# q's last 64 columns: phi before the turn, and the turn on VectorE instead of TensorE

## The chip, the core and the metric

The kernel runs on one core of one Trainium2 chip. The core has a matrix engine (TensorE, PE in the profile; PEld is its weight load), three engines for elementwise work (VectorE is DVE, ScalarE is ACT, GpSimd is POOL), and SyncE (SP), which here issues DMAs. Each engine works through its own queue in order. The metric is the time of one execution on the device in microseconds, as the median of several runs.

## The reference

`x` has 2048 tokens of 576 columns. It is normalised (layer norm without weights), and then feeds two branches whose results are combined as `x + s * silu(g)`.

```python
qkv = xn @ wqkv                       # 576 -> 3 * 576, 32 heads of 18 columns
phi = lambda t: where(t > 0, t + 1, exp(t)) + 1e-6
kv  = einsum("bhsd,bhse->bhde", phi(k), v)      # over all tokens
z   = phi(k) summed over the tokens
num = einsum("bhqd,bhde->bhqe", phi(q), kv)
den = einsum("bhqd,bhd->bhq", phi(q), z) + 1e-6
s   = (num / den) @ wo
g   = (gelu(xn @ w_gate) * (xn @ w_up)) @ w_down    # 576 -> 4608 -> 576
out = x + s * silu(g)
```

What the change touches is `phi(q)` for the last 64 of the 576 columns of q. `phi(t)` is computed as max(t, 0) + 1e-6 + exp(min(t, 0)).

## The kernel before

The 2048 tokens are four blocks of 512 (`tb` 0 to 3), a block is four tiles of 128 tokens (`TT` is 4). All is in f32; a product is made from operands that are split into a rounded word (`hi`, by ScalarE) and its remainder (`lo`, by VectorE). The work goes through these stages:

- k and v by tiles, tokens in partitions: for tile t, `x_mm` makes three products of 416, 412 and 388 columns. The last one (`TW[2]`, 388) holds 324 columns of v and, behind them, the last 64 columns of q (`Q4` is 64). `k_post` makes phi(k), `v_post` (line 486) copies v and q out of PSUM. `place(t + 1)` prepares the operands of the next tile in the midst of tile t: `normalize` (line 247) subtracts and scales on VectorE, then ScalarE writes the rounded word `xo_B` and VectorE the remainders. Every second tile, `kv_pair` accumulates kv.
- q by groups, features in partitions: q has five groups (`NHG`). Groups 0 to 3 are products over a whole block, 128 rows of q by 512 tokens. They hold 126 columns of q each, and two of the last columns as two extra rows. Group 4 is the last 64 columns. These have come out of the token tiles with tokens in partitions, so they must be turned.
- after the q of blocks 0 and 1 (called stages (tb, group) here, in the lists `behind`, line 1534) come tiles 8 to 15 of k and v, then the q of blocks 2 and 3 (lists `ahead`, line 1566), then for each block the denominators (`den`, line 753), the scaling of phi(q) by them (`scale`, `halve`) and the product with kv and `wo` (`s_mm`, line 803).
- the gated feed-forward branch, by far the longest stage, from about 240 us on.

Group 4 works like this. For each tile, `v_post` writes the 64 columns twice, side by side, into `qt[tb]` (512 tokens by 2 x 64 columns). `q_mm` with `gi == NHG - 1` lets TensorE turn the four 128x128 pieces of `qt` into one PSUM bank, so that the 64 features stand in partitions 0 to 63 and again in 64 to 127. Then `phi` (line 410) runs as for the other groups, from the bank: ScalarE takes max(-t, 0) into `e`, VectorE takes max(t, 0) + 1e-6 into `ph`, ScalarE takes the exponential of `e`, GpSimd adds.

The order within each engine is the program's order: every helper (`act` at line 123, `vec` at 126, `mm` at 129, `pool` at 132, `dma` at 135) pins its instruction. The lists `behind` and `ahead` say what is issued after each group of q. For blocks 0 and 1, phi(q) goes to DRAM (`q_store`) and is fetched again later; for blocks 2 and 3 it stays in SBUF (`q_hold`). Buffers rotate under tags: six PSUM banks (`bank`), six tiles of the tag `gl` (among them `qt` and the stored `ph`), four of the tag `tmp` (among them `e`).

For the place of things in time: block 0's group 4 is at 53 us, in tile 5; block 1's at 83 us, behind group 0 of block 0; block 2's at 178 us, behind its own group 0; block 3's at 198 us, behind its own group 0 and behind `den(2)`. The differences of operands (`difference`, names `xf_B`) run on VectorE in the stages (0,0) and (2,0), and `kv_wo` (names `kw`, `kvh`, `kvl`) in the stages (2,1) to (2,3). `den(2)` multiplies phi(q) with z on TensorE (`d`), VectorE adds and inverts (`r`), ScalarE and VectorE write the words `aux`, and `scale(2, 0, 1)` spreads them over the partitions on TensorE (`b`).

Of the kernel before, what the change touches and what calls it, by code (L numbers as in the profile page):

```python
# [8 lines left out]
F32 = mybir.dt.float32  # L9
# [3 lines left out]
ALU = mybir.AluOpType  # L13
# [3 lines left out]
P = 128  # L17
# [74 lines left out]
def block_kernel(ctx, tc, x, xe, xt, wq_d, wkv_d, wo, wgu_d, wd_d, out):  # L92
# [12 lines left out]
    def big(i, shape, dt, name):  # L105
        return sb.tile(shape, dt, tag=f"b{i}", bufs=1, name=name)
# [7 lines left out]
    def gl_tile(shape, name, dt=F32):  # L114
        return sb.tile(shape, dt, tag="gl", bufs=6, name=name)

    def tmp(shape, name):
        return sb.tile(shape, F32, tag="tmp", bufs=4, name=name)
# [3 lines left out]
    def act(*args, **kw):  # L122
        pin(nc.scalar.activation(*args, **kw))  # L123

    def vec(op, *args, **kw):
        pin(getattr(nc.vector, op)(*args, **kw))  # L126

    def mm(*args, **kw):
        pin(nc.tensor.matmul(*args, **kw))  # L129

    def pool(op, *args, **kw):
        pin(getattr(nc.gpsimd, op)(*args, **kw))  # L132

    def dma(out, in_, eng=None):
        tc.keep_in_program_order((eng or nc.sync).dma_start(out=out, in_=in_))
# [33 lines left out]
    def spread(n0, n):  # L169

        bn = sb.tile([P, TT, 12], F32, tag="bn", bufs=2, name=f"bn_{n0}")
        mv = sb.tile([P, 2 * TT, 2], F32, tag="mv", bufs=4, name=f"mv_{n0}")
        for t in range(n):
            xs = xstat[(n0 + t) // 2][:, (n0 + t) % 2]
            for j in range(2):
                src = xs[:, j, 0:HALF] if n0 < TT else xs[:, j * HALF : (j + 1) * HALF]
                vec("bn_stats", out=bn[:, t, 6 * j : 6 * j + 6], in_=src)
            vec("bn_aggr", out=mv[:, t, :], in_=bn[:, t, :])
        st = sb.tile([P, 6, TT], F32, tag="st", bufs=4, name=f"st_{n0}")
        act(st[:, 0, 0:n], mv[:, 0:n, 1], AF.Ln, bias=eps_t)  # L180
        act(st[:, 2, 0:n], st[:, 0, 0:n], AF.Exp, scale=-0.5)
        vec("tensor_scalar", st[:, 1, 0:n], mv[:, 0:n, 1], LN_EPS, None, op0=ALU.add)
        mom[n0] = n, mv, st
# [130 lines left out]
    def difference(s, i):  # L314
        f = xf[s]
        nm, a, b, o = SUMS[i]
        vec("tensor_sub", f[o], f[a], f[b])
        f[nm] = f[o]
# [79 lines left out]
    def q_part(j, i, cs):  # L398
        return wq_l[:, j, cs] if i == 4 else wq[j][:, i, cs]
# [10 lines left out]
    def phi(o, src, name):  # L410

        e = tmp(list(o.shape), f"e_{name}")
        act(e, src, AF.Relu, scale=-1.0)
        vec("tensor_scalar", o, src, 0.0, EPS, op0=ALU.max, op1=ALU.add)
        act(e, e, AF.Exp, scale=-1.0)
        pool("tensor_add", o, o, e)
# [69 lines left out]
    def v_post(t, c):  # L486

        if c == 1:
            vas[t] = slot([P, 2 * NHG, P // 2], F32, f"va_{t}")
            pool("memset", vas[t][:, :, 0:1], 1.0)  # L490
        va, src = vas[t], pkv[t, c]
        n = D - TW[0] if c == 1 else 0
        g = 4 * c - 4
        act(
            va[:, g : g + 4, 1 : GW // 2 + 1],
            src[:, n : n + 2 * GW].rearrange("p (g j) -> p g j", g=4), AF.Copy,
        )
        if c == 2:
            act(
                va[:, 8:10, 1 : W4 // 2 + 1],  # L500
                src[:, 2 * GW : 2 * GW + W4].rearrange("p (g j) -> p g j", g=2), AF.Copy,
            )
            tb, i = divmod(t, TT)
            if i == 0:
                qt[tb] = gl_tile([P, TT, 2, Q4], f"qt_{tb}")
            act(
                qt[tb][:, i], src[:, None, 2 * GW + W4 : TW[2]].to_broadcast([P, 2, Q4]), AF.Copy,
            )

    def run(todo, n=None):  # L510
        for _ in range(len(todo) if n is None else min(n, len(todo))):
# [25 lines left out]
    def kv_pair(t):  # L537

        pair = [i for i in (t - 2, t - 1) if i in vas]
        for groups in (range(4), (4,)):  # L540
            for i in pair:
                kv_mm(i, groups)
        for i in pair:
            del pks[i], vas[i]
# [3 lines left out]
    def q_mm(tb, gi, o):  # L548
        s, b = divmod(tb, 2)
        pq = bank(f"q_{tb}_{gi}")  # L550
        if gi == NHG - 1:
            t = qt.pop(tb)
            for i in range(TT):
                pin(nc.tensor.transpose(
                    pq[:, i * P : (i + 1) * P], t[:, i].rearrange("p r j -> p (r j)"), ident
                ))
        else:
            n = 0
            for j, nm in enumerate(BS[b]):
                for wi, xi, rows in PASSES:  # L560
                    mm(
                        pq, q_part(j, wi, slice(gi * P, (gi + 1) * P)), xo[s][nm][:, xi, :],
                        start=(n == 0), stop=(n == 2 * len(PASSES) - 1),
                    )
                    n += 1
        phi(o, pq, f"q{tb}_{gi}")

    def q_store(tb, gi):
        if tb not in ph_d:
            ph_d[tb] = dr.tile([P, NHG, TBN], F32, name=f"phd_{tb}")  # L570
        o = gl_tile([P, TBN], f"ph_{tb}_{gi}")
        q_mm(tb, gi, o)
        dma(out=ph_d[tb][:, gi, :], in_=o)

    def q_hold(tb, i, gi):
        if tb not in ph:
            ph[tb] = big(i, [P, NHG, TBN], F32, f"ph_{tb}")
        q_mm(tb, gi, ph[tb][:, gi, :])
# [87 lines left out]
    def kv_wo(gi):  # L666

        if gi == 4:
            at["kvh"] = big(4, [P, 4, D], F32R, "kvh")
            at["kvl"] = big(5, [P, 4, D], F32R, "kvl")  # L670

            at["kv4"] = big(6, [P, 4, D], F32R, "kv4")
            pool("memset", at["kv4"][Q4:P, 1, :].bitcast(F32), 0.0)
        kvh, kvl, kv4 = at["kvh"], at["kvl"], at["kv4"]
        zc, mh = at["zc"], at["maskh"]
        wdt, k = (W4, P // 2 + W4 // 2 + 1) if gi == 4 else (GW, P)
        w = at["wo4"] if gi == 4 else at["wo"][:, gi]
        pw = []
        for c, cs in enumerate((slice(0, HALF), slice(HALF, D + 2))):
            pw.append(bank(f"kw_{gi}_{c}"))  # L680
            mm(
                pw[c][0:wdt, 0 : cs.stop - cs.start], at["kvm"][0:k, gi, 0:wdt], w[0:k, cs],
                start=True, stop=True,
            )
        r, x_ = slice(0, Q4 if gi == 4 else GW), slice(Q4, W4)
        z = pw[1][:, HALF : HALF + 1]

        def parts(hi, lo, rows):
            for c in range(2):
                cs = slice(c * HALF, (c + 1) * HALF)  # L690
                split(hi[:, cs], lo[:, cs], pw[c][rows, 0:HALF])

        if gi == 4:
            vec("tensor_copy", zx[x_], z[x_])
            parts(kv4[x_, 2, :], kv4[x_, 3, :], x_)
            for c in range(2):
                act(kv4[Q4:P, 0, c * HALF : (c + 1) * HALF], pw[c][r, 0:HALF], AF.Copy)

        vec(
            "tensor_scalar", zc[r, gi, :], mh[r, gi, :], z[r], None, op0=ALU.mult,  # L700
        )
        if gi == 4:
            parts(kv4[r, 0, :], kv4[r, 1, :], r)
        else:
            parts(kvh[r, gi, :], kvl[r, gi, :], r)
# [773 lines left out]
    for n in range(3, 2 * TT):  # L1479
        ends = []  # L1480
        if n < 2 * TT - 2:
            ends.append(lambda n=n: x_next(n + 2))
        if n >= TT:
            j, c = divmod(n - TT, 2)
            prep_q(c, j)
            if n == TT + 1:
                load_q(1)
        if n == 2 * TT - 1:
            ends += [lambda i=i: difference(0, i) for i in range(3)]
        kv_tile(n, end=ends)  # L1490
        if n in (4, 6):
            load_x(n + 4, 2)
        if n == TT:
            for nm in BS[0]:
                keep(0, nm, xo[0][nm])
        if n == TT:
            q_store(0, 4)
        if n == TT + 3:
            keep(0, "B22", xo[0]["B22"])

# [19 lines left out]
    def form_apart(nm):  # L1520
# [12 lines left out]

    behind = {
        (0, 0): [
            lambda: kv_pair(N0), lambda: q_store(1, 4), lambda: spread(N0, 2),
            lambda: difference(0, 3),
        ],
        (0, 1): [lambda: scales(N0), lambda: form("T1")],
        (0, 2): [lambda: form_apart("T3")],  # L1540
# [8 lines left out]
    for n in range(N0, 2 * N0):  # L1549
# [13 lines left out]
        if n == 2 * N0 - 1:  # L1563
# [1 line left out]
        kv_tile(n, late_, ends)  # L1565
    ahead = {
        (2, 0): [
            lambda: kv_pair(2 * N0), kv_done, lambda: q_hold(2, 7, 4), spread_sel,
            lambda: difference(1, 3),
        ],  # L1570
        (2, 1): [lambda: kv_wo(4)],
        (2, 2): [lambda: kv_wo(0), lambda: kv_wo(1), move_rows],
        (2, 3): [lambda: kv_wo(2), lambda: kv_wo(3)],
        (3, 0): [lambda: den(2), lambda: q_hold(3, 8, 4)],
        (3, 1): [lambda: scale(2, 0, 1), lambda: halve(2, 0, 1)],
        (3, 2): [lambda: scale(2, 2, 3), lambda: halve(2, 2, 3)],
        (3, 3): [lambda: scale(2, 4), lambda: halve(2, 4)],
# [114 lines left out]
```

## Time and profile before

| | |
|---|---|
| runs | 1454.80, 1455.42, 1455.93 us; median 1455.42 us |
| profiled execution | 1454.71 us, span 1453.0 us |
| granted TensorE clock | 1.000 |
| instructions | 22169 |
| busy: PE, DVE, ACT, POOL | 1446.4, 1146.2, 565.5, 579.3 us |

Busy time by stage, from the view by stretches of time:

```profile
core 0: us, PE busy (x) PEld busy (x) DVE busy (x) ACT busy (x) POOL busy (x), PEclk, DMA share, GB/s
0.00:77.00 77.00, 75.10 (x504) 70.93 (x505) 54.19 (x135) 37.84 (x93) 28.51 (x51) 1.00 0.58 215
77.00:115.00 38.00, 37.70 (x214) 32.57 (x213) 34.60 (x55) 20.46 (x36) 14.98 (x11) 1.00 0.48 178
115.00:172.00 57.00, 56.96 (x405) 55.55 (x404) 40.47 (x100) 22.10 (x57) 16.38 (x27) 1.00 0.32 109
172.00:215.00 43.00, 42.95 (x309) 35.52 (x308) 31.87 (x55) 25.10 (x52) 19.38 (x16) 1.00 0.04 13
215.00:560.00 345.00, 345.00 (x1763) 294.93 (x1763) 247.39 (x349) 114.50 (x201) 164.62 (x136) 1.00 0.37 131
560.00:1453.00 893.00, 888.68 (x5087) 799.50 (x5085) 737.66 (x920) 345.48 (x483) 335.40 (x280) 1.00 0.54 179
```

Each line is a stretch (start and end in us from the start of the span), its length, and then for each engine its busy time and its number of instructions. Tiles 0 to 7 lie in the first stretch, the q of blocks 0 and 1 in the second, tiles 9 to 15 in the third, the q of blocks 2 and 3 in the fourth.

In a timeline, a row gives the start in us, the duration (of several instructions together, where "x" says more than one), engine, line, operation, names written and read, shapes, and in brackets the idle time of the engine before it with what ended it. In a row of a group, "busy, mean ns" come after the bar. In the view of waits, the numbers are the total in us, how often, and the longest.

### The profile page before, as it was taken

The numbers are of one execution on the slowest core, as the hardware profiler recorded it, in microseconds if no ns is written. First come the engines' busy times: TensorE is split into PE (matmuls) and PEld (weight loads), VectorE is DVE, ScalarE is ACT, GpSimd is POOL, SyncE is SP. The second block draws the span as 40 slices with busy tenths as digits, with TensorE's granted clock in tenths as the row PEclk, the third lists the DMA queues.
The fourth block names the chain that finished last, engine by engine and source line by source line (L and its number), as shares of the span: only waits on it lengthen the run. The fifth ranks groups of instructions, "written<-read, shape, count | busy, mean of one in ns | idle before, by whom it ended". The sixth has DMA issues, their size and how long they took to land.

```text
span 1453.0 us, 22169 instructions
## 1 busy us (share of the span) xinstructions
PE 1446.4 (100%) x8272; PEld 1289.0 (89%) x8272; DVE 1146.2 (79%) x1609; ACT 565.5 (39%) x918; POOL 579.3 (40%) x520
## 2 busy tenths in 40 slices
PE   9999999999999999999999999999999999999998
PEld 8989989988888888888888888888889999999998
DVE  7688667376787887887777878777878978989898
ACT  6444365333232233322332232332236555545454
POOL 3342440225756567565575755667632000000000
PEclk9999999999999999999999999999999999999999
DMA  5554115621532315224242343324289887767886
GB/s 224 187 205 152 45 42 201 225 93 51 174 102 95 130 54 186 87 95 145 77 149 87 102 145 109 113 84 136 115 277 343 265 262 254 246 183 238 277 290 224
DMA packets 119237, 235.04 MB, mean 162 GB/s; under 512 B 11658, under 2 KB 45322, under 8 KB 117210
## 3 DMA queue, kind: packets, MB, share of 16 engines
q1 hardware_dynamic: 116330, 221.37, 45.2%
q0 software_dynamic: 2656, 12.06, 2.2%
q8 instruction: 65, 1.06, 0.3%
q14 instruction: 42, 0.34, 0.1%
q10 hardware_dynamic: 144, 0.20, 0.0%
HBM read 150.96 MB, written 82.58 MB: 161 GB/s over the span
## 4 chain that ended last, share of the span: by engine, by line
PE 97%; DVE 1%; ACT 1%; issue 0%; POOL 0%; DVEq 0%; ACTq 0%; POOLq 0%
PE bd L129 25%; PE al L887 16%; PE de L887 16%; PE ga L887 16%; PE kv L129 8%; PE be L887 8%; PE s L129 4%; PE q L129 3%; PE kv_a L129 1%; PE idle L129 0%; PE d L129 0%; PE kw L129 0%; PE b L129 0%; ACT e_q L123 0%; PE xt L241 0%
## 5 line engine op out<-in xcount | busy, mean ns | idle before, releaser
L132 POOL TENSOR_TENSOR sm<-raw 128x384 f32<-128x384 f32 x72 | 75.0, 1042 | 144.3 <-DMA raw<-in_wgu_dram 113.3
L129 PE MATMUL kv<-wkv,xo_B 128*128 128x412 f32 (+2 forms) x662 | 125.0, 347 | 0.3 <-ACT xo_B L123 0.3
L129 PEld LDWEIGHTS kv<-wkv,xo_B 128*128 128x128 f32 x662 | 120.3, 188 | 1.7 <-ACT xo_B L123 0.8
L126 DVE TENSOR_TENSOR wa<-sm,wa 128x768 fp32r<-128x768 f32 x72 | 92.2, 1281 | 36.1 <-ACT wa L123 35.2
L129 PE MATMUL bd<-w_head,hi 128*128 128x288 f32 x516 | 118.0, 294 | 0.0
L126 DVE TENSOR_TENSOR wb<-raw,wb 128x256 fp32r<-128x256 f32 (+1 forms) x108 | 101.2, 937 | 7.4 <-ACT wb L123 5.8
L126 DVE TENSOR_TENSOR wa<-raw,wa 128x256 fp32r<-128x256 f32 x72 | 65.6, 911 | 50.7 <-ACT wa L123 47.5
L123 ACT ACTIVATE hi<-raw_h 128x1024 fp32r<-128x1024 f32 x59 | 62.5, 1059 | 93.0 <-PE bd L129 56.5
L129 PE MATMUL bd<-w_end,hi 128*128 128x288 f32 x448 | 89.8, 294 | 0.0
L123 ACT ACTIVATE spot_h<-spot_h 128x512 f32<-128x512 f32 x49 | 30.8, 633 | 149.4 <-DVE spot_h L126 149.4
L129 PEld LDWEIGHTS bd<-w_head,hi 128*128 128x128 f32 x516 | 87.0, 188 | 0.1
L126 DVE TENSOR_TENSOR raw_h<-raw_h,hi 128x1024 fp32r<-128x1024 f32 x59 | 71.7, 1220 | 19.1 <-ACT hi L123 18.9
L129 PE MATMUL bd<-w_end,raw_h 128*128 128x288 f32 x264 | 77.9, 295 | 0.0
L123 ACT ACTIVATE wa<-sm 128x1152 fp32r<-128x1152 f32 x36 | 41.8, 1161 | 91.1 <-PE de L887 91.1
L123 ACT ACTIVATE u<-al 128x512 f32<-128x512 f32 x72 | 41.0, 592 | 89.9 <-PE al L887 68.1
L129 PEld LDWEIGHTS bd<-w_end,hi 128*128 128x128 f32 x448 | 71.8, 188 | 0.0
L129 PE MATMUL bd<-beside,raw_h 128*128 128x288 f32 x240 | 70.8, 295 | 0.0
L132 POOL TENSOR_TENSOR spot_h<-spot_h,spot_h 128x512 f32<-128x512 f32 x45 | 62.5, 1396 | 2.9 <-DVE spot_h L126 2.4
L887 PE MATMUL al<-xo_B,wa 128*128 128x512 f32 x252 | 63.0, 389 | 0.0
L887 PE MATMUL al<-xo_B,wb 128*128 128x512 f32 x252 | 63.0, 389 | 0.0
L887 PE MATMUL be<-xo_T,wa 128*128 128x512 f32 x252 | 63.0, 389 | 0.0
L887 PE MATMUL be<-xr_T,wa 128*128 128x512 f32 x252 | 63.0, 389 | 0.0
(278 smaller groups left out, 4036.0 us busy)
## 6 DMA issues: line engine op xcount, KB each, us to landing
raw_h<-hs SPq DMA_DIRECT2D x176, 256.0 KB
raw<-in_wgu_dram SPq DMA_DIRECT2D x36, 768.0 KB
hs<-spot_h SPq DMA_DIRECT2D x90, 256.0 KB
hs<-spot_g SPq DMA_DIRECT2D x80, 256.0 KB
b<-in_wd_dram SPq DMA_DIRECT2D x42, 432.0 KB
hs<-spot_m SPq DMA_DIRECT2D x38, 256.0 KB
raw_g<-hs SPq DMA_DIRECT2D x22, 256.0 KB
raw_a<-hs SPq DMA_DIRECT2D x20, 256.0 KB
```

The costliest lines, as they stand in the source:

```text
L123: pin(nc.scalar.activation(*args, **kw))
L126: pin(getattr(nc.vector, op)(*args, **kw))
L129: pin(nc.tensor.matmul(*args, **kw))
L132: pin(getattr(nc.gpsimd, op)(*args, **kw))
L887: nc.tensor.matmul(o, w[0:rows, wi, :], xop[0:rows, xi, :], start=(start and n == 0), stop=(n == len(PASSES) - 1), skip_group_check=True,)
```

## The change

Group 4 no longer goes through TensorE.

- `v_post` writes the 64 columns once.
- `last_phi(tb)` computes phi on `qt` while the tokens still are in partitions: two VectorE operations on 128x256 in SBUF, one exponential on ScalarE, one addition on GpSimd.
- `last_turn(tb, o)` turns the result: eight VectorE transposes, for each half of 32 features and each quarter of 32 partitions, every one over the four tiles (32 partitions by 4 x 32 columns). ScalarE then copies rows 0 to 63 into rows 64 to 127.
- `last_store` and `last_hold` put the result where `q_store` and `q_hold` put it.
- The places: block 0's phi after tile 4 and its turn after tile 5 (before: both after tile 4); block 1's phi in stage (0,0) where group 4 was, and its turn at the end of that stage, behind the normalisation's sums and a difference; block 2's phi in stage (2,0) and block 3's phi at the end of that stage; block 2's turn at the end of stage (2,2), block 3's at the end of stage (2,3) (before: (2,0) and (3,0)).

```diff
@@ v_post
-                qt[tb] = gl_tile([P, TT, 2, Q4], f"qt_{tb}")
-            act(
-                qt[tb][:, i], src[:, None, 2 * GW + W4 : TW[2]].to_broadcast([P, 2, Q4]), AF.Copy,
-            )
+                qt[tb] = gl_tile([P, TT, Q4], f"qt_{tb}")
+            act(qt[tb][:, i], src[:, 2 * GW + W4 : TW[2]], AF.Copy)
@@ q_mm
-        if gi == NHG - 1:
-            t = qt.pop(tb)
-            for i in range(TT):
-                pin(nc.tensor.transpose(
-                    pq[:, i * P : (i + 1) * P], t[:, i].rearrange("p r j -> p (r j)"), ident
-                ))
...
+    def last_phi(tb):
+        t = qt[tb]
+        e = tmp([P, TT, Q4], f"e_q{tb}_l")
+        vec("tensor_scalar", e, t, 0.0, None, op0=ALU.min)
+        vec("tensor_scalar", t, t, 0.0, EPS, op0=ALU.max, op1=ALU.add)
+        act(e, e, AF.Exp)
+        pool("tensor_add", t, t, e)
+
+    def last_turn(tb, o):
+        t = qt.pop(tb)
+        cols = o.rearrange("p (i t) -> p i t", i=TT)
+        for c in range(0, Q4, 32):
+            for r in range(0, P, 32):
+                vec("transpose", cols[c : c + 32, :, r : r + 32], t[r : r + 32, :, c : c + 32])
+        act(o[Q4:P], o[0:Q4], AF.Copy)
+
+    def last_store(tb):
+        o = gl_tile([P, TBN], f"ph_{tb}_4")
+        last_turn(tb, o)
+        if tb not in ph_d:
+            ph_d[tb] = dr.tile([P, NHG, TBN], F32, name=f"phd_{tb}")
+        dma(out=ph_d[tb][:, NHG - 1, :], in_=o)
+
+    def last_hold(tb, i):
+        if tb not in ph:
+            ph[tb] = big(i, [P, NHG, TBN], F32, f"ph_{tb}")
+        last_turn(tb, ph[tb][:, NHG - 1, :])
@@ after tile n
         if n == TT:
-            q_store(0, 4)
+            last_phi(0)
+        if n == TT + 1:
+            last_store(0)
@@ behind
         (0, 0): [
-            lambda: kv_pair(N0), lambda: q_store(1, 4), lambda: spread(N0, 2),
-            lambda: difference(0, 3),
+            lambda: kv_pair(N0), lambda: last_phi(1), lambda: spread(N0, 2),
+            lambda: difference(0, 3), lambda: last_store(1),
         ],
@@ ahead
         (2, 0): [
-            lambda: kv_pair(2 * N0), kv_done, lambda: q_hold(2, 7, 4), spread_sel,
-            lambda: difference(1, 3),
+            lambda: kv_pair(2 * N0), kv_done, lambda: last_phi(2), spread_sel,
+            lambda: difference(1, 3), lambda: last_phi(3),
         ],
         (2, 1): [lambda: kv_wo(4)],
-        (2, 2): [lambda: kv_wo(0), lambda: kv_wo(1), move_rows],
-        (2, 3): [lambda: kv_wo(2), lambda: kv_wo(3)],
-        (3, 0): [lambda: den(2), lambda: q_hold(3, 8, 4)],
+        (2, 2): [lambda: kv_wo(0), lambda: kv_wo(1), move_rows, lambda: last_hold(2, 7)],
+        (2, 3): [lambda: kv_wo(2), lambda: kv_wo(3), lambda: last_hold(3, 8)],
+        (3, 0): [lambda: den(2)],
```

More of the change, by code (lines that the diff above doesn't have):

```diff
@@ L550, in q_mm @@
         pq = bank(f"q_{tb}_{gi}")
-        if gi == NHG - 1:
-            t = qt.pop(tb)
-            for i in range(TT):
-                pin(nc.tensor.transpose(
-                    pq[:, i * P : (i + 1) * P], t[:, i].rearrange("p r j -> p (r j)"), ident
-                ))
[L557 to L565, printed above, removed]
-        phi(o, pq, f"q{tb}_{gi}")
+        n = 0
+        for j, nm in enumerate(BS[b]):
+            for wi, xi, rows in PASSES:
+                mm(
+                    pq, q_part(j, wi, slice(gi * P, (gi + 1) * P)), xo[s][nm][:, xi, :],
+                    start=(n == 0), stop=(n == 2 * len(PASSES) - 1),
+                )
+                n += 1
+        phi(o, pq, f"q{tb}_{gi}")
+    def last_phi(tb):
[22 more added lines that the diff above has]
+        last_turn(tb, ph[tb][:, NHG - 1, :])
     def q_store(tb, gi):
```

## The prediction

> **What bounds the kernel now.** I read the page first, then the waits of TensorE (PE), then the timelines of the stretch that the change touches. From the page, PE's busy share and the chain that ended last:
>
> ```profile
> PE 1446.4 (100%) x8272; PEld 1289.0 (89%) x8272; DVE 1146.2 (79%) x1609; ACT 565.5 (39%) x918; POOL 579.3 (40%) x520
> ...
> PE 97%; DVE 1%; ACT 1%; issue 0%; POOL 0%; DVEq 0%; ACTq 0%; POOLq 0%
> ```
>
> PE is the whole chain, so an instruction taken off PE is worth its pitch, and work put on another engine costs nothing until PE waits for it. Where is PE near to waiting? Beyond the start, its waits have one entry, and the timeline says where:
>
> ```profile
> PE kv L129 <- ACT xo_B L123: 0.3, 1, 0.3
> ...
> 114.61 1.58 PE L129 MATMUL kv<-wkv,xo_B 128*128 128x416 f32 x7 [0.30 <-ACT xo_B L123]
> ```
>
> This is token tile 9, the first after stage (1,3). At this place PE has no slack left against what prepares its operand. I followed the preparation back (VectorE is DVE, ScalarE is ACT):
>
> ```profile
> 84.78 0.69 DVE L126 TENSOR_SCALAR ph<-q 128x512 f32<-128x512 f32 x1 [0.51 <-ACT e_q L123]
> ...
> 87.48 1.75 DVE L126 TENSOR_TENSOR xf_B<-xf_B,xf_B 128x1536 f32<-128x1536 f32 x1
> ...
> 89.14 0.68 DVE L126 TENSOR_SCALAR ph<-q 128x512 f32<-128x512 f32 x1
> ...
> 97.78 0.69 DVE L126 TENSOR_SCALAR ph<-q 128x512 f32<-128x512 f32 x1 [0.20 <-ACT e_q L123]
> ...
> 103.63 2.44 DVE L126 TENSOR_TENSOR xo_T<-xf_B,xo_T 128x1024 fp32r<-128x1024 f32 x2 [0.76 <-ACT xo_T L123]
> ```
>
> ```profile
> 100.08 0.99 ACT L123 ACTIVATE xo_B<-xf_B 128x384 fp32r<-128x384 f32 x2 [1.67 <-DVE xf_B L126]
> ...
> 108.12 0.29 ACT L123 ACTIVATE st<-mv,eps_t 128x2 f32<-128x2 f32 x1 [4.52 <-DVE mv L126]
> ...
> 114.03 1.00 ACT L123 ACTIVATE xo_B<-xf_B 128x384 fp32r<-128x384 f32 x2 [2.04 <-DVE xf_B L126]
> ```
>
> From 89 us to 114 us DVE and ACT hand one chain to and fro: where DVE idles it waits for ACT (0.76 us at 103.63), and ACT had waited for DVE just before (1.67 us at 100.08, 4.52 us at 108.12, 2.04 us at 114.03). Only the 0.20 us at 97.78 hangs on PE through `e_q`. A delay of DVE at 89 us therefore reaches PE at 114.61 less 0.20 us.
>
> The second tight place is the denominator of block 2, which PE computes (`d`), DVE inverts into `aux`, and PE spreads (`b`):
>
> ```profile
> 181.11 1.76 DVE L126 TENSOR_TENSOR xf_B<-xf_B,xf_B 128x1536 f32<-128x1536 f32 x1
> ...
> 189.23 1.02 DVE L126 TENSOR_TENSOR kvl<-kw,kvh 126x288 fp32r<-126x288 f32 x2
> ...
> 192.21 0.69 DVE L126 TENSOR_SCALAR ph<-q 128x512 f32<-128x512 f32 x1 [1.97 <-ACT e_q L123]
> ...
> 194.30 1.02 DVE L126 TENSOR_TENSOR kvl<-kw,kvh 126x288 fp32r<-126x288 f32 x2
> ...
> 197.38 0.69 DVE L126 TENSOR_SCALAR ph<-q 128x512 f32<-128x512 f32 x1 [2.06 <-ACT e_q L123]
> ...
> 199.69 1.28 DVE L126 TENSOR_TENSOR aux<-r,aux 32x128 fp32r<-32x128 f32 x4 [0.44 <-ACT aux L123]
> ```
>
> ```profile
> 182.22 0.60 ACT L123 ACTIVATE e_q<-q 128x512 f32<-128x512 f32 x1 [0.41 <-PE q L129]
> ...
> 186.40 0.60 ACT L123 ACTIVATE e_q<-q 128x512 f32<-128x512 f32 x1 [0.47 <-PE q L129]
> ```
>
> ```profile
> 201.50 0.62 PE L129 MATMUL b<-aux 128*128 128x512 f32 x2
> ...
> 208.98 0.29 PE L129 MATMUL s<-kvh,pq 128*128 128x288 f32 x1
> ```
>
> `aux` is ready at 199.69 + 1.28 = 200.97, and PE takes it at 201.50: 0.53 us of slack.
>
> **What leaves PE.** Sixteen turns; PE's own duration overstates them, the starts of the weight loads give the pitch:
>
> ```profile
> L554 PE MATMUL q<-ident,qt x16: 270/272/329, 53.4 to 198.2; 128*128 128x128 f32 x16
> ```
>
> ```profile
> 53.18 0.54 PEld L554 LDWEIGHTS q<-ident,qt 128*128 128x128 f32 x4
> ...
> 53.68 0.49 PEld L129 LDWEIGHTS kv<-wkv,xo_B 128*128 128x128 f32 x3
> ```
>
> ```profile
> 178.28 0.42 PEld L554 LDWEIGHTS q<-ident,qt 128*128 128x128 f32 x4
> ...
> 178.67 0.30 PEld L129 LDWEIGHTS q<-xo_B,wq 128*128 128x128 f32 x2
> ```
>
> Four turns hold PE 0.50 us in block 0 and 0.39 us in block 2; with blocks 1 and 3 taken like block 2 that is 1.7 us in all, the most that the change can gain.
>
> **What comes to the others, with prices.**
>
> ```profile
> 52.39 0.32 DVE L126 TENSOR_SCALAR e_k<-kv 128x160 f32<-128x160 f32 x1
> 52.63 0.31 DVE L126 TENSOR_SCALAR pk<-kv 128x160 f32<-128x160 f32 x1
> ```
>
> ```profile
> 164.88 0.28 DVE L126 TENSOR_TENSOR xo_B<-xf_B,xo_B 32x128 fp32r<-32x128 f32 x1
> ...
> 114.59 0.42 DVE L126 TENSOR_TENSOR xo_B<-xf_B,xo_B 128x256 fp32r<-128x256 f32 x1
> ...
> L126 DVE TENSOR_SCALAR x<-x,mv,st 128x768 f32<-128x768 f32 x4 | 2.7, 680 | 0.1
> ```
>
> ```profile
> 82.96 0.63 ACT L123 ACTIVATE e_q<-e_q 128x512 f32<-128x512 f32 x1
> ...
> 53.34 0.36 ACT L123 ACTIVATE va<-kv 128x252 f32<-128x252 f32 x1
> ...
>   ACT e_q L123: 7.5, 11
> ```
>
> - The eight turns of a block, t together. No row has one; the nearest by shape is 32x128, 0.28 us, which gives t = 2.24 us, and I take it. Low end: two neighbours that overlap start 0.24 us apart at 0.32 us of duration, 0.08 us saved at each of seven joints: 1.68 us. High end: a block is filled and drained one after the other, as if there were 256 columns, 0.42 us each: 3.36 us.
> - phi in rows: two operations on 128x256 for one of 0.69 us from PSUM. 128x768 in SBUF took 0.68 us and 32x128 0.28 us, so I take 0.33 us each: 0.66 us, nil against the 0.69 us. If each takes 0.42 us, DVE is 0.15 us later per block.
> - ACT's two passes over 128x512 (0.60 and 0.63 us) become one over 128x256 (0.36 us by the 128x252 row) and the doubling copy, 64x512, at 0.63 us like 128x512. `qt` is written sixteen times with half the columns; a smaller write can't cost more, and I count it at nil. POOL adds half the elements and nobody in the two chains waits for it.
> - The new wait. The doubling copy stands in ACT's queue behind the turns, and in front of the `e_q` of the next group of q. DVE's `ph` starts only after that `e_q` (the last row above, from the view of the tile `q`: 7.5 us in 11 waits). So a block's turns cost DVE t + 0.10 (hand-over) + 0.63 + 0.60 + 0.06 = t + 1.39 us until the next `ph`, less the idle time that was there.
>
> The rows for the queues, SP's fetch of the moments and ACT's use of them:
>
> ```profile
> 94.91 0.32 SPq L135 DMA_DIRECT2D mx<-md  x1
> ...
> 110.86 1.13 ACT L123 ACTIVATE mr<-mx 128x512 f32<-128x512 f32 x1
> ```
>
> The store of block 1 moves from behind phi to behind the difference; its DMA stays on SP's queue, where behind it wait other stores, which nobody near needs, and the moments of tiles 8 and 9, fetched at 94.91 and used at 110.86: 16 us of cover, so nil; without it tile 9's operand would be late by the delay. The hold of blocks 2 and 3 issues no DMA.
>
> **Block 0.** DVE's waits in the tile after the turns:
>
> ```profile
> 64.55 0.59 DVE L126 TENSOR_SCALAR e_k<-kv 128x416 f32<-128x416 f32 x1 [1.66 <-PE kv L129]
> ...
> 65.95 0.59 DVE L126 TENSOR_SCALAR pk<-kv 128x416 f32<-128x416 f32 x1 [0.81 <-PE kv_a L129]
> ```
>
> This block (around 53 to 66 us) is covered: DVE idles 1.66 us for PE at tile 6 and 0.81 us behind it, together more than t. Without that cover its t would be on the path to tile 7's operand.
>
> **Block 1, first place.** PE and so all that feeds on it comes 0.50 us earlier, and the 0.51 us for block 1's `e_q` goes, since `qt` is ready early. The difference that ended at 87.48 + 1.75 = 89.23 ends at 88.22. Then turns, copy and `e_q`: next `ph` at 88.22 + t + 1.39 = 91.85 against 89.14, 2.71 us late; 0.20 us is absorbed. PE goes on 2.5 us later than before at 114.61, and the 0.9 us that PE gained by then is spent in the wait.
>
> **Blocks 2 and 3, second place** (times as before the change, with that shift left out). Block 3's phi now stands behind the difference that ended at 182.87, and its exponential in ACT's queue ahead of `e_q`: 182.87 + 0.33 + 0.09 + 0.36 + 0.60 + 0.03 = 184.28 against 182.82, 1.46 us late; ACT's 0.47 us of waiting for PE at 186.40 absorbs part, so 0.99 us stays and `kvl` ends at 191.24 instead of 190.25. Block 2's turns: next `ph` at 191.24 + t + 1.39 = 194.87 against 192.21, 2.66 us late. The next `kvl` ends at 195.32 + 2.66 = 197.98; block 3's turns: `ph` at 201.61 against 197.38, 4.23 us late. `aux` is ready at 205.20, and `b` starts at 205.25, 3.75 us after 201.50, though PE without eight turns would be there at 200.72. Behind `b` PE has 7.5 us of other work (201.50 to 208.98) before `s` needs DVE's scaled words, so nothing is lost twice; and PE has no later wait that could take it back.
>
> **Sum.** 2.5 + 3.75 = 6.25 us; in terms of t it is 3t - 0.46 (once in the first place, twice in the second): 4.6 us at t = 1.68, 9.6 us at 3.36. Against the profiled execution (1454.71 us, span 1453.0) that is 1461.0; against the median of the runs, 1455.42, it is 1461.6. Their spread is 1454.80 to 1455.93; what a measurement can tell is about 0.2%, 2.9 us.
>
> **The skill against the rows.** The row pair at 52.39 shows two neighbours overlapping by 0.08 us. The Trainium skill, "VectorE: DVE Perf Modes", section "Two Vector instructions with no wait between them", says that an instruction whose input starts in another group of 32 partitions than the last one's is held until all earlier ones have finished; the eight turns change the group each time, so by it they do not overlap and t is 2.24, not 1.68. No run here shows a turn yet. The same page of the Trainium skill, section "The three transpose paths", gives 311 ns for VectorE over 128x128 in bf16, and under "Rules for kernel authors" it sends a full 128x128 turn to TensorE; as an estimate from that figure t would be 2.49 us and the time 1462.4.
>
> **Rivals.**
> - Hidden, not slower. If `ph` did not truly need `e_q` first (the wait could be the record's choice, both following PE), the copy would cost the chain nothing, and the first place would cost t - 1.12 us, the second nothing up to about t = 1.1. It decides at 0.14 us a turn. Then PE keeps what it gained: down to 1455.42 - 1.7 = 1453.7. For it: PE waits nowhere else. Against: in all four rows of `ph` with idle time above, `e_q` ended it and never PE; and 0.14 us is half of the nearest row.
> - Half bitten. With that free wait but t = 2.24, the first place costs 1.1 and the second 1.0 us: 1457.5, not to be told from no change.
> - One place only. If the lateness in the (2,0) stage is made up by ACT and the first place is absorbed, 1455.42 + 3.75 = 1459.2.
> - Dear turns, t = 3.36: 1465.0.
>
> **Chances.** The forecast 0.50 (its own range 1459.5 to 1463), dear turns 0.13, one place only 0.13, half bitten 0.14, hidden 0.10. Slower by over 0.2% (above 1458.3): 0.50 + 0.13 + 0.13 = 0.76. Within 0.2%: half bitten and nearly all of hidden, 0.22. Faster by over 0.2%: 0.02, since PE has only 1.7 us to give. The range 1457.0 to 1465.2 leaves out hidden and the upper tail of dear turns.
>
> **What would show it.** Turns near 0.28 us in DVE's groups, not overlapping; PE's wait for `xo_B` at tile 9 grown from 0.30 to about 3.7 us (2.5 plus the 0.9 gained); a new wait of PE `b` for DVE `aux` of some 4.5 us; ACT's copy ahead of `e_q` with idle time put down to DVE. Wrong, if `ph` starts before the copy ends, if a turn is far from 0.28 us, or if PE waits elsewhere.

## The result and the profile after

The changed kernel takes 1465.42 us (median of 4 runs, 1464.16 to 1466.22), the kernel before 1455.51 us beside it. The ratio is 1.0067, 95% interval 1.0055 to 1.0079: slower by 9.9 us. The forecast was slower, 1461.6 us, in a range up to 1465.2 us. So the sign held, and the size was missed by 3.8 us. The profiled execution after is the longest of the four: it took 1466.22 us, span 1464.5 us, granted TensorE clock 0.996.

PE's line of the page, and PE's waits in the kernel after (total, times, longest, in us). Before, the only such wait beyond the start was 0.3 us at `kv`:

```profile
PE 1450.7 (99%) x8256; PEld 1290.2 (88%) x8256; DVE 1160.0 (79%) x1645; ACT 563.7 (38%) x918; POOL 578.2 (39%) x520
```

```profile
PE b L129 <- DVE aux L126: 4.0, 1, 4.0
PE ms L233 <- DVE st L126: 2.3, 1, 2.3
...
PE kv L129 <- ACT xo_B L123: 0.6, 1, 0.6
PE kw L129 <- DVE kv L126: 0.4, 1, 0.4
```

Both forecast places are there, `kv` (tile 9) and `b`. `ms` is a new one, and so is a small one at `kw`. The timeline of PE after shows where they stand and what follows them:

```profile
95.29 0.32 PE L233 MATMUL ms<-ident,st 128*128 128x128 f32 x1 [2.35 <-DVE st L126]
95.39 2.23 PE L129 MATMUL q<-xo_B,wq 128*128 128x512 f32 x5
...
118.29 10.62 PE L129 MATMUL kv<-wkv,xo_B 128*128 128x416 f32 x56 [0.61 <-ACT xo_B L123]
...
209.20 1.19 PE L129 MATMUL b<-aux 128*128 128x512 f32 x2 [4.00 <-DVE aux L126]
210.19 2.33 PE L129 MATMUL q<-xo_B,wq 128*128 128x512 f32 x5
...
219.58 0.42 PE L129 MATMUL s<-kvh,pq 128*128 128x288 f32 x2
```

Tile 9 starts at 118.29 us instead of 114.61 (3.68 us later), `b` at 209.20 instead of 201.50 (7.70 later, so 4.02 us more), `s` at 219.58 instead of 208.98 (10.60 later, so 2.90 us more). Look at the five q matmuls behind each wait: 2.23 and 2.33 us. Before the change the same fives took 1.39 and 1.30 us:

```profile
93.62 1.39 PE L129 MATMUL q<-xo_B,wq 128*128 128x512 f32 x5
...
201.95 1.30 PE L129 MATMUL q<-xo_B,wq 128*128 128x512 f32 x5
```

The view by stretches, after, gives the granted clock for those two places (PEclk, the third number from the end) and, between them, for a stretch behind the short wait at tile 9:

```profile
95.00:100.00 5.00, 4.71 (x14) 3.77 (x15) 4.86 (x8) 3.62 (x6) 2.03 (x2) 0.66 0.19 64
118.00:129.00 11.00, 10.71 (x60) 10.38 (x62) 9.11 (x25) 6.46 (x14) 3.00 (x4) 1.00 0.48 165
209.00:216.00 7.00, 6.80 (x18) 5.39 (x19) 3.32 (x6) 2.25 (x5) 1.29 (x1) 0.56 0.00 0
```

Before the change the clock was 1.00 in every stretch of the table by stage. Behind the waits at `ms` and `b`, TensorE was granted 0.66 and 0.56 of it, as means over these stretches.

VectorE after, with the group of the turns first (busy us, mean ns), then its timeline in both places, and ScalarE's and GpSimd's row that belong to them:

```profile
L126 DVE STREAM_TRANSPOSE ph<-qt 32x128 f32<-32x128 f32 x32 | 9.6, 300 | 0.4
```

```profile
83.75 0.28 DVE L126 TENSOR_SCALAR e_q_l<-qt 128x256 f32<-128x256 f32 x1
84.07 1.35 DVE L126 TENSOR_SCALAR qt<-qt 128x256 f32<-128x256 f32 x1
...
89.10 2.50 DVE L126 STREAM_TRANSPOSE ph<-qt 32x128 f32<-32x128 f32 x8
92.92 0.69 DVE L126 TENSOR_SCALAR ph<-q 128x512 f32<-128x512 f32 x1 [1.32 <-ACT e_q L123]
...
194.88 2.50 DVE L126 STREAM_TRANSPOSE ph<-qt 32x128 f32<-32x128 f32 x8
198.70 0.69 DVE L126 TENSOR_SCALAR ph<-q 128x512 f32<-128x512 f32 x1 [1.32 <-ACT e_q L123]
...
201.71 2.49 DVE L126 STREAM_TRANSPOSE ph<-qt 32x128 f32<-32x128 f32 x8
205.53 0.69 DVE L126 TENSOR_SCALAR ph<-q 128x512 f32<-128x512 f32 x1 [1.32 <-ACT e_q L123]
```

```profile
91.63 0.63 ACT L123 ACTIVATE ph<-ph 64x512 f32<-64x512 f32 x1 [3.74 <-DVE ph L126]
```

```profile
83.98 1.29 POOL L132 TENSOR_TENSOR ph<-ph,e_q 128x512 f32<-128x512 f32 x1 [4.10 <-DVE ph L126]
```

Eight turns take 2.50 us, 0.31 us each with no overlap. Behind them VectorE idles 1.32 us, three times, until ScalarE has made the copy (0.63 us) and the next `e_q`. And in block 1 the maximum on `qt` took 1.35 us, while the minimum just before it, on the same shape, took 0.28 us; it ended about when GpSimd's addition did (83.98 + 1.29 = 85.27).

From here the feed-forward stage starts 10.6 us late (its first product at 287.21 us instead of 276.60), and the span ends 11.5 us late. In the rest of 0.9 us PE has one wait of 0.4 us that was not there before (at `ga`). The profiles of two experiments (fill, and blocks 0 to 2 in gaps) show the like and the others don't; its cause stays open.

### The profile page after: what moved, and what is told of

Same layout as the page of the kernel before. It is cut to its first block, busy times and chain, and to the rows that moved or that the text cites. A ratio compares the mean times of both kernels' runs of the same rounds, so it can differ in the third digit from the quotient of the medians.

```text
span 1464.5 us, 22175 instructions
## 1 busy us (share of the span) xinstructions
PE 1450.7 (99%) x8256; PEld 1290.2 (88%) x8256; DVE 1160.0 (79%) x1645; ACT 563.7 (38%) x918; POOL 578.2 (39%) x520
## 4 chain that ended last, share of the span: by engine, by line
PE 94%; DVE 4%; ACT 1%; issue 1%; POOL 0%; DVEq 0%; ACTq 0%; POOLq 0%
PE bd L129 25%; PE ga L906 16%; PE de L906 16%; PE al L906 15%; PE kv L129 8%; PE be L906 8%; PE s L129 4%; DVE ph L126 1%; PE q L129 1%; DVE xf_B L126 1%; ACT e_q L123 1%; PE kv_a L129 1%; DVE xo_T L126 0%; PE idle L129 0%; PE b L129 0%
## 5 line engine op out<-in xcount | busy, mean ns | idle before, releaser
L906 PE MATMUL ga<-xo_B,wb 128*128 128x512 f32 x252 | 63.3, 390 | 0.4 <-DVE u L126 0.4
L906 PE MATMUL ga<-xr_B,wb 128*128 128x512 f32 x252 | 63.0, 389 | 0.0
L906 PE MATMUL al<-xr_B,wa 128*128 128x512 f32 x252 | 63.0, 389 | 0.0
```

Of the source, the lines that this page charges most:

```text
L906: nc.tensor.matmul(o, w[0:rows, wi, :], xop[0:rows, xi, :], start=(start and n == 0), stop=(n == len(PASSES) - 1), skip_group_check=True,)
```

## The experiments

The theory after this reading: three terms that add up. First, block 1's turns delay tile 9 (3.7 us). Second, the turns of blocks 2 and 3 make PE wait at `b` (4.0 us). Third, the clock is lower behind that wait (2.9 us). The rivals stand with each run. Two experiments restore a part (with the lines below go the double write of `qt` and the turns in `q_mm` for those blocks):

```diff
 # block 1 by TensorE again               # blocks 2 and 3 by TensorE again
-  last_phi(1) ... last_store(1)          -  last_phi(2), last_phi(3), last_hold(2, 7), last_hold(3, 8)
+  q_store(1, 4)                          +  q_hold(2, 7, 4), q_hold(3, 8, 4)
```

Block 1 back:

> Block 1 goes back to TensorE's turns, blocks 0, 2 and 3 stay on VectorE. Theory: the loss is three terms that add up, 3.7 us at tile 9 (block 1's turns), 4.0 us of wait at PE b (blocks 2 and 3) and 2.9 us of slow clock behind that wait. Without the first, about 1461.5 us, PE's wait for DVE st before ms gone, its wait at b still near 4 us. Rival: the second place is late only because the first one left VectorE behind; then the wait at b shrinks too, and the time is 1456 to 1458 us.

Blocks 2 and 3 back:

> Blocks 2 and 3 go back to TensorE's turns, blocks 0 and 1 stay on VectorE. Theory: only the first term is left, about 1459.2 us, with PE's waits before ms (2.3 us) and at tile 9 (0.6 us) as they were and none at b. Rival (one chain through both places): the first place's lateness is made up by 172 us, and the time is within 1 us of 1455.5.

The third fills PE's wait (its 16 products are extra work that nothing reads):

```diff
     def scale(tb, *gs):
+        if tb == 2 and gs[0] == 0:
+            o = own_bank("fill")
+            for _ in range(16):
+                mm(o, q_part(0, 0, slice(0, P)), xo[1]["B12"][:, 0, :], start=True, stop=True)
```

> As after the change, but PE runs 16 matmuls of q's shape into a bank that nobody reads, ahead of the first b of block 2 (about 3.6 us of the 4.0 us that it waits there). Theory: the slow matmuls behind the wait come from the granted clock, which falls because PE idles; kept busy, PE stays at full clock, the stretch from b to the first s is 7.5 us as before the change instead of 10.4, and the time is about 1462.5 us. Rival: the matmuls behind b are slow for another reason (their operands, banks not yet free), then it stays 1465.4 us or gets worse.

The fourth moves the copies:

```diff
-        act(o[Q4:P], o[0:Q4], AF.Copy)            # in last_turn, for blocks 1, 2, 3
+        (0, 1): [lambda: last_put(1), ...]        # copy and store, behind phi of group 1
+        (2, 3): [lambda: double(ph[2][:, NHG - 1, :]), ...]
+        (3, 0): [lambda: den(2), lambda: double(ph[3][:, NHG - 1, :])]
```

> The doubling copies of blocks 1, 2 and 3 stand behind the phi of the next group of q in ScalarE's queue instead of ahead of it; turns and all else as after the change. Theory: each place loses the 1.32 us that VectorE idled there; the first place costs 2.4 us instead of 3.7, the wait at b falls from 4.0 to about 1.4 us and is then too short to cost clock: about 1458.5 us. Rival: the turns' own time on VectorE is the price and the copy only fills time that would be idle; then within 1 us of 1465.4 us.

Measured, and the starts in the profiles (us) of tile 9, of the first `b`, of the first `s`, of the first product of the feed-forward stage, and the span. Later runs are in the same table:

| kernel | median us | ratio to before, interval | tile 9 | b | s | feed-forward | span |
|---|---|---|---|---|---|---|---|
| before | 1455.51 | | 114.61 | 201.50 | 208.98 | 276.60 | 1453.0 |
| after | 1465.42 | 1.0067, 1.0055 to 1.0079 | 118.29 | 209.20 | 219.58 | 287.21 | 1464.5 |
| block 1 back | 1461.11 | 1.0039, 1.0025 to 1.0054 | 114.33 | 205.20 | 215.13 | 282.77 | 1459.3 |
| blocks 2, 3 back | 1459.52 | 1.0025, 1.0014 to 1.0036 | 118.64 | 206.73 | 214.21 | 281.83 | 1458.2 |
| fill | 1463.63 | 1.0057, 1.0042 to 1.0072 | 118.42 | 210.68 | 218.28 | 285.90 | 1463.1 |
| late copy | 1459.98 | 1.0028, 1.0017 to 1.0040 | 117.13 | 206.82 | 214.42 | 282.05 | 1458.5 |
| phi 1 early | 1464.48 | 1.0066, 1.0051 to 1.0081 | 118.68 | 209.62 | 218.79 | 286.41 | 1462.7 |
| only block 0 | 1454.60 | 0.9998, 0.9989 to 1.0007 | 114.49 | 201.34 | 208.82 | 276.44 | 1452.8 |
| all in gaps | 1457.54 | 1.0019, 1.0010 to 1.0028 | 114.09 | 201.09 | 208.69 | 278.37 | 1455.8 |
| 0 to 2 in gaps | 1455.27 | 0.9996, 0.9987 to 1.0005 | 114.36 | 200.73 | 208.21 | 275.85 | 1453.6 |

*The two places are independent.* The two medians, 1461.11 and 1459.52 us, lie near what the sum of terms gave (1461.5 and 1459.2 us), and neither rival came true. With block 1 back, PE's wait at `b` is 4.00 us as in the changed kernel, tile 9 is in time, and `ms` does not wait:

```profile
114.33 10.65 PE L130 MATMUL kv<-wkv,xo_B 128*128 128x416 f32 x56 [0.30 <-ACT xo_B L124]
...
205.20 1.19 PE L130 MATMUL b<-aux 128*128 128x512 f32 x2 [4.00 <-DVE aux L127]
```

With blocks 2 and 3 back, the wait at `b` is gone, and the lateness of tile 9 stays to the end. Here PE's timeline and the clock behind the wait at tile 9:

```profile
95.66 0.32 PE L234 MATMUL ms<-ident,st 128*128 128x128 f32 x1 [2.35 <-DVE st L127]
95.76 1.39 PE L130 MATMUL q<-xo_B,wq 128*128 128x512 f32 x5
...
118.64 12.21 PE L130 MATMUL kv<-wkv,xo_B 128*128 128x416 f32 x56 [2.20 <-ACT xo_B L124]
```

```profile
118.60:131.00 12.40, 12.36 (x62) 11.88 (x64) 9.10 (x24) 6.57 (x14) 2.97 (x4) 0.86 0.43 146
```

Here the wait of 2.35 us at `ms` left the clock alone (1.39 us for five matmuls), so PE came to tile 9 earlier, waited 2.20 us instead of 0.61, and lost the clock there: the 56 matmuls took 12.21 us instead of 10.62. That was not expected: the wait at tile 9 was to stay 0.6 us. Tile 9 starts in both profiles when VectorE's chain lets it. So the slow matmuls behind `ms` cost nothing, and those behind tile 9 cost 1.6 us.

*The clock.* With the fill, PE's idle time at `b` shrinks to 0.38 us, and what follows runs at full speed:

```profile
206.51 3.79 PE L129 MATMUL fill<-xo_B,wq 128*128 128x512 f32 x16
210.68 0.70 PE L129 MATMUL b<-aux 128*128 128x512 f32 x2 [0.38 <-DVE aux L126]
211.22 1.32 PE L129 MATMUL q<-xo_B,wq 128*128 128x512 f32 x5
```

```profile
209.00:220.00 11.00, 10.62 (x53) 8.77 (x51) 8.64 (x16) 7.29 (x14) 2.94 (x4) 1.00 0.01 1
```

From `b` to `s` it is 7.60 us for the same products, against 10.38 us after the change and 7.48 us before. That shows the third term: PE's idle time of 4 us cost 2.8 us more in clock in this pair of profiles. The size varies: with the same wait, `b` to `s` took 9.93 us with block 1 back and 9.17 us with block 1's phi early (below), so against 7.48 us the clock cost 2.45 and 1.69 us there, and 2.90 us after the change. The median fell by 1.8 us, of about 2.9 expected, and the intervals of the two ratios overlap, so the profile shows this term and the median alone does not. The profile also says why the gain can be short: the wait at tile 9 was 2.16 us, and its 56 matmuls took 12.17 us. This kernel and the changed one are the same program up to `b`, so where the clock falls after waits of 2 us differs between executions.

*The copy's place in the queue.* With late copies VectorE's `ph` follows the turns at once, tile 9 starts at 117.13 us, and the wait at `b` falls to 1.44 us, without loss of clock (7.60 us from `b` to `s`):

```profile
89.24 2.50 DVE L126 STREAM_TRANSPOSE ph<-qt 32x128 f32<-32x128 f32 x8
91.77 0.69 DVE L126 TENSOR_SCALAR ph<-q 128x512 f32<-128x512 f32 x1
```

```profile
206.82 0.70 PE L129 MATMUL b<-aux 128*128 128x512 f32 x2 [1.44 <-DVE aux L126]
```

5.4 us came back, of 6.9 expected; 1.5 us is lost in clock at tile 9, which was not expected (2.16 us of wait, 12.17 us for the 56 matmuls).

The fifth run asks what made 1.35 us of a 0.3 us operation:

```diff
-            lambda: kv_pair(N0), lambda: last_phi(1), lambda: spread(N0, 2),
+            lambda: kv_pair(N0), lambda: spread(N0, 2),
+        if n == 2 * TT - 1:
+            last_phi(1)
```

> As after the change, but block 1's phi stands behind tile 7, ahead of group 0 of block 0, where GpSimd is idle. Theory: the 1.35 us that VectorE's maximum on qt took in block 1 (0.30 us in block 0) was 1.05 us of waiting for GpSimd's addition running beside it; it takes 0.30 us here, tile 9 starts 1 us earlier (about 117.3 us), and the time is about 1464.4 us. Rival: the operation is slow for its own operands; then 1.35 us again and 1465.4 us.

The timeline of VectorE in that kernel, and GpSimd's addition to `qt`:

```profile
84.20 0.30 DVE L126 TENSOR_SCALAR qt<-qt 128x256 f32<-128x256 f32 x1
85.14 0.69 DVE L126 TENSOR_SCALAR ph<-q 128x512 f32<-128x512 f32 x1 [0.64 <-ACT e_q L123]
```

```profile
84.70 0.74 POOL L132 TENSOR_TENSOR qt<-qt,e_q_l 128x256 f32<-128x256 f32 x1 [4.09 <-ACT e_q_l L123]
```

GpSimd is idle until 84.70 us, and without it beside it the operation takes 0.30 us, so it was the neighbour and not the operands. But 0.64 us of the gain became a wait for `e_q`, which now stands behind block 1's exponential. Tile 9 came no earlier: this execution was 0.7 us later at the first q matmul, in the start-up, and counted from there tile 9 came 0.33 us earlier than in the changed kernel, not the 1 us expected. The time can't be told from the changed kernel's.

The last three ask whether the change can be had without its price. Only block 0 by VectorE:

> Only block 0 is turned by VectorE, blocks 1 to 3 by TensorE as before the change. Theory: block 0's turns lie in idle time of VectorE, so this is the one part without a price: PE reaches tile 6 about 0.5 us earlier, and the time is 1455.0 to 1455.6 us, with PE's wait at tile 9 up to 0.8 us at most. Rival: block 0 is late too and pays a part of the loss: above 1456.5 us.

1454.60 us, which can't be told from no change. No wait is new, and the feed-forward stage starts 0.16 us earlier. That agrees with the forecast's block 0: covered, and worth 0.5 us at most.

All four blocks, each turn put where VectorE waits for PE (to make room for block 1's own tile, two small tiles are also made smaller):

```diff
+        if n == 2 * TT - 1:                      # block 1's phi
+            last_phi(1)
+        if n == N0 + 4:                          # block 1's turn, behind tile 12; its qt in a tile of its own
+            last_store(1)
+        (2, 2): [..., half_turn(2, row(2, 7), 0)]
+        (2, 3): [half_turn(2, row(2, 7), 1), double(row(2, 7)), kv_wo(2), kv_wo(3), last_phi(3)]
+        (3, 0): [den(2), half_turn(3, row(3, 8), 0)]
+        (3, 1): [scale(2, 0, 1), halve(2, 0, 1), half_turn(3, row(3, 8), 1), double(row(3, 8))]
```

> All four blocks by VectorE, but each turn where VectorE waits for TensorE: block 1's phi behind tile 7 and its turn behind tile 12 (its qt in a tile of its own), block 2's turn in two halves at the ends of stage (2,2) and at the start of (2,3), block 3's phi at the end of (2,3) and its turn in halves behind den(2) and at the end of (3,1), the copies behind them. Theory: the price of the change is only where the work stands; no new wait of PE above 0.5 us, full clock throughout, PE keeps most of its 1.7 us: about 1454.0 us. Rival: 4 x 2.5 us of turns cannot be hidden in this stretch wherever they stand; then 1457 us or more.

1457.54 us, so the rival's number came true and not the 1454.0 us expected. The place at tile 9 is mended (114.09 us, earlier than before the change). PE waits for the reciprocals and, for the first time, for the scaled words:

```profile
201.09 0.70 PE L129 MATMUL b<-aux 128*128 128x512 f32 x2 [0.81 <-DVE aux L126]
...
214.13 0.79 PE L129 MATMUL s<-kv,pq 128*128 128x288 f32 x4 [1.86 <-DVE pq L126]
```

The wait at `b` costs nothing against the kernel before, since `b` starts 0.41 us earlier than there. The wait at `s` is the loss: the feed-forward stage starts 1.77 us late. VectorE's and ScalarE's rows ahead of it:

```profile
205.52 1.25 DVE L126 STREAM_TRANSPOSE ph<-qt 32x128 f32<-32x128 f32 x4
208.09 0.69 DVE L126 TENSOR_SCALAR ph<-q 128x512 f32<-128x512 f32 x1 [1.32 <-ACT e_q L123]
```

```profile
206.80 0.63 ACT L123 ACTIVATE ph<-ph 64x512 f32<-64x512 f32 x1 [2.03 <-DVE ph L126]
```

The second half of block 3's turn has the copy behind it, ahead of the next `e_q`, and VectorE idles the same 1.32 us as in the changed kernel. So these rows put much of the loss on the copy's place again, and not on the turn alone. That the turns can't be hidden wherever they stand, as the rival has it, is not shown; block 3 with a later copy was not run.

The same without block 3 (and with block 2's copy one place later):

> Block 3 by TensorE as before the change, block 0 as after it, block 1's phi behind tile 7 and its turn behind tile 12, block 2's turn in two halves at the end of stage (2,2) and the start of (2,3) with the copy behind a part of kv_wo. Theory: in the run with all four blocks in gaps, block 3's turn was what no longer fitted (waits of 0.8 us at b and 1.9 us at s); without it there is no new wait of PE, and PE keeps 0.5 + 0.4 + 0.4 us: 1453.9 us, a ratio near 0.999. Rival: what VectorE gains in idle time is taken back by later waits in these stretches too; then 1455.2 us or more.

1455.27 us, which can't be told from no change. The interval holds both the ratio expected (0.999) and the rival's, so the median decides nothing between them. In its profile the feed-forward stage starts 0.75 us before that of the kernel before, where 1.3 us was expected. Then the stage takes 1.35 us longer than before, and one wait in it is 0.6 us of that; the rest was not traced:

```profile
PE ga L935 <- DVE u L127: 0.6, 1, 0.6
```

No version that beats the kernel before by more than the measurement was found; in the best case there were 1.7 us to win.

## Why the prediction was right in sign and short in size

- *What leaves PE: 1.7 us.* No run shows the whole of it. At the start of the feed-forward stage the gain was 0.16 us with block 0 alone (0.5 forecast) and 0.75 us with three blocks in gaps (1.3 by the same pitches).
- *The turns, t = 2.24 us.* Measured 2.50 us, 0.31 each. The low end fell, since they don't overlap, and so did the high end. The Trainium skill's rule that a VectorE instruction whose input starts in another group of 32 partitions than the last one's is held until the earlier ones have finished ("VectorE: DVE Perf Modes", "Two Vector instructions with no wait between them") agrees with this trace, eight turns in 2.50 us at 0.30 us each. The estimate of 2.49 us from the figure of the Trainium skill's "The three transpose paths" ("VectorE: DVE Perf Modes") comes out near too, though that figure is for another shape and type, so the agreement may be luck.
- *The new wait behind the copy, 1.39 us.* Measured 1.32 us idle, three times, and shown by the late copies. The rivals "hidden" and "half bitten", which needed `ph` to be free of the copy, are out; "one place only" is out by the two runs that restore a part.
- *phi in rows, nil.* True for blocks 0 and 2 (0.28 to 0.30 us an operation), wrong for block 1: 1.05 us were missed, since the operation took that much longer beside GpSimd's addition. Block 3's two operations were slow as well (0.83 us at 186.15 us and 0.69 us at 187.01 us), with GpSimd at work from 184.77 to 188.33 us. The effect was to be read in the rows before the change, where one and the same operation took 0.16 us and, beside GpSimd's addition, 1.15 us:

```profile
55.95 0.16 DVE L126 SCALAR_TENSOR_TENSOR st<-st 128x2 f32<-128x2 f32 x1
...
90.13 1.15 DVE L126 SCALAR_TENSOR_TENSOR st<-st 128x2 f32<-128x2 f32 x1
```

```profile
89.97 1.29 POOL L132 TENSOR_TENSOR ph<-ph,e_q 128x512 f32<-128x512 f32 x1 [3.02 <-DVE st L126]
```

  The Trainium skill, "GPSIMD Engine Reference", "Specifications", names this contention, between GpSimd and VectorE's 2-port modes or instructions with two SBUF inputs; the 1.35 against 0.30 us agree.
- *First place, 2.5 us.* Measured 3.68 us. By the rows the difference is the 1.05 us above and 0.26 us of turns, less 0.07 us of the shorter wait behind the copy. The wait of `ms` was not foreseen; in this profile it cost nothing, as VectorE's chain set the start of tile 9 anyway.
- *Second place, 3.75 us.* Measured 4.02 us, with 4.00 us of wait at `b` (4.5 forecast). This chain was read rightly: less the 3.68 us of the first place, block 2's turn started at 191.20 us (191.24 forecast).
- *"Behind `b` PE has 7.5 us of other work, so nothing is lost twice."* This is the step that failed. The work was there, but it took 10.38 us, as the granted clock had fallen in the 4 us of waiting. These 2.9 us (2.45 and 1.69 us in two other profiles with the same wait) are the largest part of what was missed: 6.25 forecast, and 3.68 + 4.02 + 2.90 = 10.6 us measured at the feed-forward stage. The waits were priced at their length, and not at what the clock does behind them.
- *The rival "dear turns"* gave 1465.0 us, nearly the result, for a reason that is false: the turns cost 2.50 and not 3.36 us.

## What to carry to other kernels

Price a wait of TensorE at its length and then ask what the clock does behind it: here 4.0 us of waiting cost 1.7 to 2.9 us more. When work goes from the busiest engine to a less busy one, follow the chain that the other engine carries, since VectorE with 79% busy time had two chains with 0.2 and 0.5 us to spare. The place in a queue can decide more than the busy time: moving three copies gave 5.4 us back. A small copy in an in-order queue, ahead of the operation that another engine waits for, cost more than half as much as the eight turns themselves (1.32 against 2.50 us), and it could stand one place later.

## What the runs showed of the hardware that was not expected

- The granted clock fell after waits as short as 2.2 us, but not after each: after 2.35 us at `ms` it fell in the changed kernel's profile (0.66 over 95 to 100 us) and not with blocks 2 and 3 back or with the fill (five matmuls in 1.39 us); after 2.16 to 2.20 us at tile 9 it fell in three profiles (12.2 us for 56 matmuls instead of 10.6), and after 2.15 us with block 1's phi early it did not (10.61 us). After 1.44 us at `b` it did not fall. After 4.0 us it fell each time, and the stretch from `b` to `s` took 10.38, 9.93 and 9.17 us instead of 7.48. The Trainium skill, "TensorE: Matmul & The Clock Gate", "What's actually happening", has the clock fall after an idle window of about 3.4 us that runs freely. That would fit the spread after 4.0 us, which no run here tests; the falls after 2.2 us are behind waits shorter than that window, and there the measurement decides.
- A VectorE operation of 0.30 us took 1.35 us beside GpSimd's addition of 1.29 us, and 0.30 us again with GpSimd idle.
